# Attention and gated MLP on one core: one SBUF pool for raw q, k, v and for the weight conversions, with two weight pieces and part of x's sums moved beside the last two pairs

## The chip, the core and the metric

The kernel runs on one core of a Trainium2 chip. The metric is the device time of one execution in microseconds (us). The core has a matrix engine (PE, with its weight loads listed as PEld), a vector engine (DVE), an activation engine (ACT), a general engine (POOL) and SP, which here only issues DMA transfers. Each engine works through its own queue in order. Numbers of a profile come from one profiled execution; times are medians over several runs.

## What is computed

The reference has two parts. Attention over 8 images and 8 heads, 576 tokens and 64 channels per head, with a mask by blocks of 64; then a gated MLP over all 4608 tokens:

```python
scores = scale * np.matmul(q, k.transpose(0, 1, 3, 2))
mask = block_i >= block_j
scores = np.where(mask, scores, -1000000000.0)
scores = scores - np.max(scores, axis=-1, keepdims=True)
attn = np.exp(scores)
attn = attn / (np.sum(attn, axis=-1, keepdims=True) + 1e-09)
attn_out = np.matmul(attn, v)
x = attn_out.transpose(0, 2, 1, 3).reshape(B * S, H * D)      # 4608 x 512
gate = 1.0 / (1.0 + np.exp(-(x @ w_gate)))
out = gate * (x @ w_val) @ w_out                              # 512 -> 1536 -> 512
```

The three weights come in as 64-bit floats, q, k and v as 32-bit floats.

## The kernel before

**Arithmetic.** Wide products run in a rounded 32-bit format (F32R in the code). To keep precision, most operands are held as a high part and a low part (H and L in names), the high part by a copy that rounds, the low part by a subtraction; a product then takes three matmuls: high by high, high by low, low by high.

**Weights.** A 64-bit weight arrives as two 32-bit words (`raw`). `to_f32` (lines 650 to 673) makes a 32-bit float `cT` of them by integer operations on DVE: lines 659, 666, 668, 670, 672 and 673, with a mask of the small values made on ACT by a square (line 665), or on DVE (line 662) where the flag `alone` is set. `combine` (line 683) then forms sums of four weight blocks (lines 694 to 697) and splits them into high (ACT, line 698) and low parts (DVE, line 699). `wo_piece` (line 702) does the same for the output weights, without sums, and splits at lines 708 and 709. One call of either is a "piece"; a unit of weights, such as (0, 0) or (0, 1), has two pieces.

**First stage: attention and the first four of twelve hidden chunks.** 32 pairs (an image and two heads), numbered 0 to 31, run one after the other, in a software pipeline written out by hand (the loop at line 574): in its step p, the scores and softmax of pair p run beside the second half (transposes, product with v) of pair p-1 and `prep`, which loads and transposes q and k, of pair p+1. `convert` works off weight pieces for this stage, and `mlp1` computes the first four hidden chunks of an image whose attention is done; its matmuls are mixed into PE's queue by a rate. The loop has one step more than pairs: in step 32 only the second half of pair 31 is left. Then `run(mlp)` (line 829) works off what is left of `mlp1`, which for the last image, image 7, is nearly all. A tick is one part of such a step; p = 31 has some 22 of them.

**Second stage: the other eight hidden chunks.** It runs in two groups g of four hidden chunks, and within a group over k = 0 to 5, blocks of 768 tokens. The two products by w_gate and w_val use seven block products in place of eight (Strassen's scheme, in `unit`), so that x, too, has to be brought in as seven sums: `x_fetch` (line 711) loads four blocks of x from DRAM into `XB` (line 723) and makes three sums and, in slot 6, a fourth (lines 727 to 730), on DVE for the first block and on POOL for the others; `x_split` (lines 735 to 740) makes high (ACT, line 738) and low (DVE, line 739) parts in `XO`, the tiles `XH` and `XL`. `unit` issues the block products (line 749) and DVE and ACT clear the results (lines 765 to 793), with the low part of the hidden values at line 757. `out_block` multiplies by the output weights (line 807), and adds, in the second group, what the earlier parts left in DRAM (lines 821 to 824). Four units of 42 matmuls and an output part of 72 matmuls make a block.

**Order around the change.** The tile framework takes the program as written, adds every wait that data need, and orders each engine's queue by its own planner's simulation. `behind(a, b)` forces a after b on the same queue without a wait. Before, in the order of the program:

1. the loop over pairs ends, and the attention's pool `at` closes;
2. the pools `x2` (first weights, XO) and `cv` (raw weights, `cT`, `XB`) open, on the memory of `at`;
3. `combine` of unit (0, 0), both pieces (line 826), `x_fetch` and `x_split` of block 0 (line 827);
4. `run(mlp)`, whose first multiplication on DVE (line 135) is put behind the sums of step 3 (`first_sums`, lines 826 to 828, used at line 518);
5. `combine` of units (0, 1), (1, 0), (1, 1), then four pieces of the output weights, in the order 0, 2, 1, 3;
6. the loop over g and k, which fetches the x of the next block at its head.

In the first stage the raw rows of q, k and v lie in `rq`, `rk` and `rv`, the transposed ones in a buffer with the tag T, the split q in two tiles `QS0` and `QS1` by turns, and the keys in two buffers of `KD`. All of these belong to `at`. The low parts of k are made at line 251, on POOL from pair 1 on; a pair's keys then go to the other half of the partitions by a transfer within SBUF (line 252).

Of the kernel before, what the change touches and what calls it, by code (L numbers as in the profile page):

```python
# [9 lines left out]
F32 = mybir.dt.float32  # L10
# [8 lines left out]
F1 = 4  # L19
# [10 lines left out]
def attn_glu_kernel(ctx: ExitStack, tc: tile.TileContext, q, k, v, w_gate, w_val, w_out, out):  # L30
# [118 lines left out]
    with ExitStack() as s2:  # L149
        s1 = ExitStack()  # L150
        s_at = ExitStack()
        mp, xp1, wp1, xp0 = (s1.enter_context(tc.tile_pool(name=x, bufs=1, side="left")) for x in ("m1", "x1", "w1", "x0"))
        at = s_at.enter_context(tc.tile_pool(name="at", bufs=1, side="right"))
# [19 lines left out]
        QSs = [at.tile([P, 2, 640], F32R, name=f"QS{i}") for i in range(2)]  # L173
# [67 lines left out]
        def prep(p):  # L241


            KD = at.tile([P, 2, 2, S], F32R, name="KD", bufs=2)
            QS = QSs[p % 2]
            kT = at.tile([P, S], F32, name="kT", tag="T", bufs=1)
# [7 lines left out]
            qT = at.tile([P, S], F32, name="qT", tag="T", bufs=1)  # L254
# [304 lines left out]

        n = len(pairs)  # L560
# [12 lines left out]

        for p in range(n + 1):
            pr = prep(p + 1) if p + 1 < n else iter(())
# [11 lines left out]
            for g, what in plan:  # L587
# [7 lines left out]
                for _ in part:  # L595
# [9 lines left out]
                    convert_to(p, min(1.0, tick / 20))  # L605
            convert_to(p, 1.0)
# [12 lines left out]

        W_OF = {1: 0, 5: 1, 2: 2, 4: 3, 7: 4, 6: 5, 3: 6}
        X_OF = {1: 0, 7: 1, 2: 2, 3: 3, 5: 4, 6: 5, 4: 6}
        G = (NF - F1) // 4
        NK = NTOK // (2 * N2)
        KC = NC // 2
        def pool(name, **kw):  # L630
            return s2.enter_context(tc.tile_pool(name=name, bufs=1, side="right", reuse_waits="tile", **kw))
        units = [(q, gv) for q in range(2) for gv in range(2)]

        s_at.close()
        x2 = pool("x2")
        cv = pool("cv")
        wp = {(0, 0): x2}
        wgv_d = dram.tile([4, P, KC, 2, 7, P], F32, name="wgv_d")
        wo_d = dram.tile([P, 4, 2, DM], F32, name="wo_d")
        part2_d = dram.tile([NTOK, DM], F32, name="part2_d")  # L640
        last2 = {}

        def mark2(engine, ins):
            last2[engine] = ins.ins
# [6 lines left out]

        def to_f32(raw, T_, sq, held, alone=False):

            def after(engine, ins):
                if held and engine in last2:
                    behind(ins.ins, last2[engine])
            lo, hi = raw[:, :, 0], raw[:, :, 1]
            Tu = T_.bitcast(U32)
            after("DVE", nc.vector.tensor_scalar(out=Tu, in0=hi, scalar1=3, scalar2=0x3FFFFFF8,
                                                 op0=ALU.logical_shift_left, op1=ALU.bitwise_and))  # L660
            if alone:
                nc.vector.tensor_scalar(out=sq.bitcast(U32), in0=hi, scalar1=0x7FFFFFFF, scalar2=None,
                                        op0=ALU.bitwise_and)
            else:
                after("ACT", nc.scalar.activation(out=sq, in_=hi.bitcast(F32), func=AF.Square))
            nc.vector.scalar_tensor_tensor(out=Tu, in0=hi, scalar=0xC0000000, in1=Tu,
                                           op0=ALU.bitwise_and, op1=ALU.bitwise_or)
            nc.vector.scalar_tensor_tensor(out=T_, in0=sq, scalar=TINY_HI if alone else TINY_HI * TINY_HI, in1=T_,
                                           op0=ALU.is_ge, op1=ALU.mult)
            nc.vector.tensor_scalar(out=hi, in0=Tu, scalar1=0xFF800000, scalar2=None, op0=ALU.bitwise_and)  # L670
            Ef = hi.bitcast(F32)
# [253 lines left out]
```

## Time and profile before

| | us |
|---|---|
| median of 3 runs | 1315.14 (1311.15 to 1316.25) |
| the profiled execution | 1313.64 |
| its span, first to last instruction | 1311.8 |
| stage 1 with the attention's last work (the last x parts of pair 31 made) | to about 681 |
| first block product of the second stage | 731.1 |

The profile gives each engine's busy time, a chain of waits followed back from the last instruction, groups of instructions by source line with mean durations in ns, and, on request, instructions in order of time. In rows of the latter the first number is the start, the second the length, then the engine, the line of the kernel, the operation, and what it writes and reads (`out<-in`), with the count of merged instructions; idle time just before it stands in brackets with what ended it. SPq is SP's queue of transfer issues. A row of a chain has start, length and work.

For the whole span:

```profile
PE   5879899999999999999997969999999999999997
DVE  7899988989899898898849996887887757556643
PEclk8989989999999999999998979999999999999999
```

Each digit is a slice of a fortieth of the span, in tenths of busy time, or of full clock.

### The profile page before, as it was taken

The numbers are of one execution on the slowest core, as the hardware profiler recorded it, in microseconds if no ns is written. First come the engines' busy times: TensorE is split into PE (matmuls) and PEld (weight loads), VectorE is DVE, ScalarE is ACT, GpSimd is POOL, SyncE is SP. The second block draws the span as 40 slices with busy tenths as digits, with TensorE's granted clock in tenths as the row PEclk, the third lists the DMA queues.
The fourth block names the chain that finished last, engine by engine and source line by source line (L and its number), as shares of the span: only waits on it lengthen the run. The fifth ranks groups of instructions, "written<-read, shape, count | busy, mean of one in ns | idle before, by whom it ended". The sixth has DMA issues, their size and how long they took to land.

```text
span 1311.8 us, 21661 instructions
## 1 busy us (share of the span) xinstructions
PE 1226.5 (93%) x7312; PEld 1132.2 (86%) x7312; DVE 1044.9 (80%) x2097; ACT 781.0 (60%) x1871; POOL 506.8 (39%) x490
## 2 busy tenths in 40 slices
PE   5879899999999999999997969999999999999997
PEld 4668779989899898999997959899899999999996
DVE  7899988989899898898849996887887757556643
ACT  5877768888888888888855433444445324223320
POOL 2313344535545355454520134313322415624531
PEclk8989989999999999999998979999999999999999
DMA  7656535354454544544232334423528632542442
GB/s 144 141 122 137 123 80 130 79 128 92 88 123 83 125 91 102 113 82 114 70 94 78 121 120 166 141 92 138 173 85 315 234 96 98 193 152 74 161 145 97
DMA packets 256959, 161.87 MB, mean 123 GB/s; under 512 B 197328, under 2 KB 217808, under 8 KB 256208
## 3 DMA queue, kind: packets, MB, share of 16 engines
q1 hardware_dynamic: 255248, 157.53, 44.4%
q10 hardware_dynamic: 1600, 2.95, 0.6%
q8 instruction: 58, 0.95, 0.3%
q14 instruction: 53, 0.43, 0.1%
HBM read 94.37 MB, written 47.19 MB: 108 GB/s over the span
## 4 chain that ended last, share of the span: by engine, by line
PE 57%; DVE 24%; ACT 8%; DMA 6%; issue 3%; SPq 1%; POOL 0%; DVEq 0%; POOLq 0%; ACTq 0%
PE b L749 21%; PE bank L222 10%; PE m L114 6%; PE m L807 6%; PE m L123 5%; PE bank L225 3%; PE b L807 3%; DVE QS L260 2%; DVE P L371 2%; DVE XL L739 2%; DMA part_d<-ost 2%; ACT P L316 2%; DVE nm L324 2%; DMA rq<-in_q_dram 1%; PE bank L114 1%
## 5 line engine op out<-in xcount | busy, mean ns | idle before, releaser
L749 PE MATMUL b<-XH,w 128*128 128x384 f32 x1344 | 353.7, 339 | 12.2 <-ACT XH L738 6.7
L749 PEld LDWEIGHTS b<-XH,w 128*128 128x128 f32 x1344 | 245.8, 189 | 20.1 <-ACT XH L738 7.9
L749 PE MATMUL b<-XL,w 128*128 128x384 f32 x672 | 226.4, 337 | 1.3 <-DVE XL L739 1.3
L222 PE MATMUL bank<-KD,QS 128*128 128x288 f32 (+4 forms) x768 | 160.7, 332 | 17.0 <-DMA KD<-KD 11.3
L316 ACT ACTIVATE P<-bank,nm 128x512 f32<-128x512 f32 (+3 forms) x256 | 134.1, 528 | 29.4 <-DVE nm L324 18.4
L222 PEld LDWEIGHTS bank<-KD,QS 128*128 128x128 f32 x768 | 117.9, 197 | 26.1 <-DVE QS L260 11.3
L251 POOL TENSOR_TENSOR KD<-kT,KD 64x576 fp32r<-64x576 f32 x62 | 91.1, 1470 | 113.5 <-ACT KD L250 111.1
L749 PEld LDWEIGHTS b<-XL,w 128*128 128x128 f32 x672 | 127.1, 189 | 3.6 <-DVE XL L739 1.8
L807 PE MATMUL m<-wo,hH 128*128 128x512 f32 x384 | 125.4, 392 | 0.0
L225 PE MATMUL bank<-ident,P 128*128 128x128 f32 x640 | 96.3, 282 | 18.9 <-DVE P L371 10.9
L114 PE MATMUL m<-XH,wv 128*128 128x288 f32 x448 | 106.9, 305 | 3.8 <-DVE h L135 3.8
L822 POOL TENSOR_TENSOR pr<-pr,pr 128x512 f32<-128x512 f32 x36 | 46.9, 1305 | 156.6 <-DMA pr<-part_d 155.8
L114 PE MATMUL m<-XH,wg 128*128 128x288 f32 x448 | 105.3, 304 | 0.6 <-ACT t L133 0.5
L225 PEld LDWEIGHTS bank<-ident,P 128*128 128x128 f32 x640 | 76.2, 144 | 26.9 <-ACT P L316 14.5
L222 PE MATMUL bank<-G1H,VS 128*128 128x320 f32 (+2 forms) x352 | 95.6, 355 | 1.8 <-ACT G1H L295 1.8
L371 DVE TENSOR_SCALAR P<-P,sm 128x512 f32<-128x512 f32 (+3 forms) x256 | 91.2, 414 | 1.0
L807 PEld LDWEIGHTS m<-wo,hH 128*128 128x128 f32 x384 | 72.3, 189 | 13.8
L297 DVE TENSOR_TENSOR G1L<-bank,G1H 128x512 fp32r<-128x512 f32 (+1 forms) x120 | 74.2, 622 | 12.0 <-ACT G1H L295 11.5
L772 ACT ACTIVATE g<-g 128x384 f32<-128x384 f32 x72 | 37.0, 524 | 77.2 <-DVE g L785 66.5
L114 PEld LDWEIGHTS m<-XH,wv 128*128 128x128 f32 x448 | 76.8, 190 | 4.8 <-DVE h L135 4.6
L114 PEld LDWEIGHTS m<-XH,wg 128*128 128x128 f32 x448 | 76.5, 190 | 1.6 <-ACT t L133 1.3
L324 DVE TENSOR_REDUCE nm<-bank 128x1 f32<-128x384 f32 (+1 forms) x128 | 76.3, 603 | 0.8
(181 smaller groups left out, 3103.1 us busy)
## 6 DMA issues: line engine op xcount, KB each, us to landing
KD<-KD SPq DMA_DIRECT2D x64, 288.0 KB, 3.1
pr<-part_d SPq DMA_DIRECT2D x72, 256.0 KB, 3.6
part_d<-ost SPq DMA_DIRECT2D x60, 256.0 KB, 3.0
rk<-in_k_dram SPq DMA_DIRECT2D x128, 72.0 KB, 2.5
XB<-xT_d SPq DMA_DIRECT2D x16, 576.0 KB, 5.3
out_dram<-ost SPq DMA_DIRECT2D x36, 256.0 KB, 2.9
xT_d<-xT SPq DMA_DIRECT2D x30, 288.0 KB, 2.3
rv<-in_v_dram SPq DMA_DIRECT2D x64, 128.0 KB, 2.8
```

Source lines behind the costliest of these rows:

```text
L114: mm = nc.tensor.matmul(ps, lhsT=lh, rhs=rh, start=(i == 0), stop=(i == n - 1))
L123: mm = nc.tensor.matmul(ps, lhsT=lh[:, f, t * P:(t + 1) * P], rhs=rh, start=(i == 0), stop=(i == n - 1))
L222: pe_last[:] = [nc.tensor.matmul(*args, **kw).ins]
L225: pe_last[:] = [nc.tensor.transpose(*args).ins]
L251: (nc.gpsimd if p else nc.vector).tensor_sub(out=KD[s, h, 1], in0=kT[s], in1=KD[s, h, 0].bitcast(F32))
L297: mark("DVE", nc.vector.tensor_sub(out=dst[1], in0=src, in1=dst[0].bitcast(F32)))
L316: mark("ACT", nc.scalar.activation(out=Pi[:, h], in_=ps, func=AF.Exp, bias=nm[:, c0 + h:c0 + h + 1], accum_out=sm[:, c0 + h:c0 + h + 1]))
L324: mark("DVE", nc.vector.tensor_reduce(out=nm[:, c0 + h:c0 + h + 1], in_=ps, axis=AX.X, op=ALU.max, negate=True))
L371: mark("DVE", nc.vector.tensor_scalar_mul(Pi[:, h], Pi[:, h], sm[:, c0 + h:c0 + h + 1]))
L749: mm = nc.tensor.matmul(ps, lhsT=lh, rhs=rh, start=(first and k == 0), stop=(k == n - 1), skip_group_check=not first)
L807: mm = nc.tensor.matmul(po[t], lhsT=lh[:, f, t * P:(t + 1) * P], rhs=rh, start=(half == 0 and i == 0), stop=(half == 1 and i == 5))
L822: nc.gpsimd.tensor_add(out=pr[0], in0=pr[0], in1=pr[1])
```

## The change

Raw q, k, v, the transposed ones, `QS` and `KD` move from `at` into a pool `cv` that opens before `at` and stays for the rest of the kernel; there they are `rqk` (raw q and k), `rvT` (raw v, and behind it the transposed k or q), `QS0`, `QS1` and `KD`. The second stage's `raw` takes by turns the tags of `QS0` and `QS1`, its `cT` those of `rqk` and `rvT`, and `XB`, with six slots in place of seven, that of `KD`. The helpers that need them are defined before the loop over pairs. With that:

- at the start of steps 31 and 32 the raw words of one piece of unit (0, 0) and one half of block 0's x are fetched; the sums of the first piece are made at tick 20 of step 31, x's first three sums at tick 1 of step 32, the sums of the second piece at tick 4 of step 32, each behind the last marked DVE instruction of the attention;
- after the loop come the sums of x's second half, the splitting of the two pieces, high part now on DVE, and then fetch and sums of unit (0, 1), its mask on DVE; the low parts of block 0's x are put behind these; line 135's first multiplication waits in order only for the sums of x's second half;
- x's slot 6 is no longer made with the sums: `x_split` subtracts in place on DVE in slot 2, after slots 0 to 3 have been split, and splits in three parts in place of two;
- block 1's x is loaded after unit (0, 1) has been split, and its sums are made on DVE, behind the last instruction of unit (1, 0); later blocks' sums stay on POOL.

```diff
+        cv = s2.enter_context(tc.tile_pool(name="cv", bufs=1, side="right", reuse_waits="tile"))
...
-        rq = at.tile([P, S], F32, name="rq")
-        rk = at.tile([P, S], F32, name="rk")
-        rv = at.tile([P, 5, P], F32, name="rv")
+        rqk = cv.tile([P, 2, S], F32, name="rqk")
+        rq, rk = rqk[:, 0], rqk[:, 1]
+        rvT = cv.tile([P, 5 * P + S], F32, name="rvT")
+        rv, qkT = rvT[:, :5 * P].rearrange("p (t d) -> p t d", d=P), rvT[:, 5 * P:]
...
-        QSs = [at.tile([P, 2, 640], F32R, name=f"QS{i}") for i in range(2)]
+        QSs = [cv.tile([P, 2, 640], F32R, name=f"QS{i}") for i in range(2)]
...
-            KD = at.tile([P, 2, 2, S], F32R, name="KD", bufs=2)
+            KD = cv.tile([P, 2, 2, S], F32R, name="KD", bufs=2)
...
-            kT = at.tile([P, S], F32, name="kT", tag="T", bufs=1)
+            kT = qT = qkT
...
+        def cv_tiles():
+
+            i = n_cv[0] % 2
+            n_cv[0] += 1
+            return (cv.tile([P, 4 * P, 2], U32, name="raw", tag=f"QS{i}"),
+                    cv.tile([P, 8, P], F32, name="cT", tag=("rqk", "rvT")[i]))
...
+        def split_gv(T, dst, alone=False):
+            if alone:
+                nc.vector.tensor_copy(out=dst[:, 0], in_=T[:, :7])
+            else:
+                nc.scalar.copy(out=dst[:, 0], in_=T[:, :7])
+            return nc.vector.tensor_sub(out=dst[:, 1], in0=T[:, :7], in1=dst[:, 0].bitcast(F32)).ins
...
+        def x_load(k, j):
...
+            XB = cv.tile([P, 6, N2], F32, name="XB", tag="KD", bufs=2)
...
+        def x_sums(XB, eng, other=None):
+            t1 = eng.tensor_sub(out=XB[:, 4], in0=XB[:, 1], in1=XB[:, 0])
+            if other:
+                behind(t1.ins, other)
+            eng.tensor_sub(out=XB[:, 1], in0=XB[:, 3], in1=XB[:, 1])
+            return eng.tensor_sub(out=XB[:, 5], in0=XB[:, 3], in1=XB[:, 4]).ins
+
+        def x_split(XBs, other=None):
+
+            def split(a, b, src):
+                for j, XB in enumerate(XBs):
+                    if src == 2:
+                        nc.vector.tensor_sub(out=XB[:, 2], in0=XB[:, 2], in1=XB[:, 5])
+                    x = XB[:, src:src + b - a]
+                    nc.scalar.copy(out=XO[j][0][:, a:b], in_=x)
+                    sub = nc.vector.tensor_sub(out=XO[j][1][:, a:b], in0=x, in1=XO[j][0][:, a:b].bitcast(F32))
+                    if other:
+                        behind(sub.ins, other)
+
+            split(0, 4, 0)
+            split(4, 6, 4)
+            split(6, 7, 2)
...
+        def early_work(p, tick):
+
+            when = p - (n - 1), tick
+            if when in ((0, 0), (1, 0)):
+                early.append(fetch_gv(0, 0, 0, len(early)))
+                early_x.append(x_load(0, len(early_x)))
+            if when == (0, 20):
+                sums_gv(*early[0], alone=last["DVE"])
+            if when == (1, 1):
+                x_sums(early_x[0], nc.vector, last["DVE"])
+            if when == (1, 4):
+                sums_gv(*early[1], alone=last["DVE"])
...
-        first_sums = [combine(0, 0, 0, j, W[0, 0][:, j], alone=True) for j in range(KC)]
-        x_split(x_fetch(0, nc.vector))
-        first_sums.append(last2["T4"])
+        first_sums = [x_sums(early_x[1], nc.vector)]
+        for j in range(KC):
+            done = split_gv(early[j][1], W[0, 0][:, j], True)
+        early = [fetch_gv(0, 0, 1, j) for j in range(KC)]
+        for e in early:
+            sums = sums_gv(*e, alone=done)
+        x_split(early_x, sums)
         run(mlp)
...
-        for q, gv in units[1:]:
+        for n, (q, gv) in enumerate(units[1:]):
             for j in range(KC):
-                combine(0, q, gv, j, W[q, gv][:, j])
+                if n:
+                    done = combine(0, q, gv, j, W[q, gv][:, j])
+                else:
+                    split_gv(early[j][1], W[q, gv][:, j])
+            if n == 1:
+                sums_after = done
+            if n == 0:
+                XBs = [x_load(1, j) for j in range(KC)]
         for f in (0, 2, 1, 3):
             wo_piece(0, f, wo[:, f])
+        for XB in XBs:
+            x_sums(XB, nc.vector, sums_after)
...
-                if not end:
-                    XBs = x_fetch((k + 1) % NK, nc.gpsimd)
+                if not end and (g or k):
+                    XBs = [x_load((k + 1) % NK, j) for j in range(KC)]
+                    for XB in XBs:
+                        x_sums(XB, nc.gpsimd)
```

`fetch_gv` and `sums_gv` are the fetching and summing parts of the former `combine`, `early_work` is called at the head of each step and after each tick.

More of the change, by code (lines that the diff above doesn't have):

```diff
@@ L558, in mlp1, with pool @@
                         queue.dma_start(out=part_d[r:r + 64, :], in_=ost[64 * j:64 * j + 64, :])
+        W_OF = {1: 0, 5: 1, 2: 2, 4: 3, 7: 4, 6: 5, 3: 6}
+        X_OF = {1: 0, 7: 1, 2: 2, 3: 3, 5: 4, 6: 5, 4: 6}
+        G = (NF - F1) // 4
+        NK = NTOK // (2 * N2)
+        KC = NC // 2
+        def pool(name, **kw):
+            return s2.enter_context(tc.tile_pool(name=name, bufs=1, side="right", reuse_waits="tile", **kw))
+        units = [(q, gv) for q in range(2) for gv in range(2)]
@@ new lines, in fetch @@
+        def fetch(raw, src, held):
+            for dst, x in zip(raw, src):
+                d = nc.sync.dma_start(out=dst, in_=x.bitcast(U32))
+                if held:
+                    behind(d.ins, last2["SP"])
+                else:
+                    mark2("SP", d)
+        n_cv = [0]
+        def cv_tiles():
[3 more added lines that the diff above has]
+                    cv.tile([P, 8, P], F32, name="cT", tag=("rqk", "rvT")[i]))
@@ new lines, in x_load @@
+        def x_load(k, j):
+            b, o = divmod(2 * k * N2, S)
+            n0 = S - o
+            XB = cv.tile([P, 6, N2], F32, name="XB", tag="KD", bufs=2)
+            v = XB[:, 0:4].rearrange("p (kh th) n -> p kh (th n)", kh=2)
+            src = xT_d.rearrange("b (kh c p) s -> c b p kh s", kh=2, c=KC)[j]
+            for dst, x in ((v[:, :, :n0], src[b][:, :, o:]), (v[:, :, n0:], src[b + 1][:, :, :2 * N2 - n0])):
+                d = nc.sync.dma_start(out=dst, in_=x)
+                if "SP" in last2:
+                    behind(d.ins, last2["SP"])
+                mark2("SP", d)
+            return XB
@@ L650, in attn_glu_kernel @@
         XO = [[x2.tile([P, 7, N2], F32R, name=f"X{e}{j}") for e in "HL"] for j in range(KC)]
[L652 to L671, printed above, removed]
-            nc.vector.scalar_tensor_tensor(out=Ef, in0=lo, scalar=2.0 ** -52, in1=Ef, op0=ALU.mult, op1=ALU.mult)
-            nc.vector.tensor_add(out=T_, in0=T_, in1=Ef)
@@ L735, in x_split @@
-        def x_split(XBs):
-            for a, b in ((0, 4), (4, 7)):
-                for j, XB in enumerate(XBs):
-                    nc.scalar.copy(out=XO[j][0][:, a:b], in_=XB[:, a:b])
-                    nc.vector.tensor_sub(out=XO[j][1][:, a:b], in0=XB[:, a:b],
-                                         in1=XO[j][0][:, a:b].bitcast(F32))
         def product(i, ps, w, first):
```

127 lines of the change are left out of this document (58 added, 69 removed).

## The prediction

> **What bounds the kernel now.** I read the page's busy times and chain first, then busy time by stage, then PE's timeline in the stages where PE is not full.
>
> ```profile
> PE 1226.5 (93%) x7312; PEld 1132.2 (86%) x7312; DVE 1044.9 (80%) x2097; ACT 781.0 (60%) x1871; POOL 506.8 (39%) x490
> PE 57%; DVE 24%; ACT 8%; DMA 6%; issue 3%; SPq 1%; POOL 0%; DVEq 0%; POOLq 0%; ACTq 0%
> 660.00:676.00 16.00, 16.00 (x114) 15.29 (x114) 9.99 (x25) 9.83 (x27) 5.22 (x6) 1.00 0.11 36
> 676.00:687.00 11.00, 11.00 (x63) 9.76 (x62) 0.69 (x2) 3.51 (x7) 2.16 (x2) 1.00 0.63 184
> 687.00:731.00 44.00, 35.99 (x217) 33.43 (x216) 40.15 (x89) 21.67 (x37) 0.00 (x0) 0.92 0.32 107
> 731.00:790.00 59.00, 48.63 (x236) 44.39 (x235) 58.34 (x89) 25.14 (x41) 19.61 (x15) 0.88 0.35 115
> 790.00:835.00 45.00, 44.66 (x233) 41.09 (x232) 34.52 (x55) 19.61 (x34) 13.47 (x12) 1.00 0.35 115
> ```
>
> In the stage rows the columns after the length are PE, PEld, DVE, ACT and POOL busy, then PE's granted clock and the DMA share. PE is full at 660-687 and 790-835. It is not between: there DVE is full (58.34 of 59.00), straight after it did almost nothing for 11 us (0.69). So over the change's place DVE sets the pace. PE's timeline shows the price, the idle time in brackets:
>
> ```profile
> 703.02 0.61 PE L114 MATMUL bank<-XH,wg 128*128 128x288 f32 x1 [8.01 <-DVE h L135]
> 760.63 0.44 PE L749 MATMUL b<-XH,w 128*128 128x384 f32 x1 [2.22 <-DVE g L785]
> 773.47 0.44 PE L749 MATMUL b<-XH,w 128*128 128x384 f32 x1 [3.42 <-ACT XH L738]
> 776.96 1.33 PE L749 MATMUL b<-XH,w 128*128 128x384 f32 x3 [3.05 <-ACT XH L738]
> 782.05 0.69 PE L749 MATMUL b<-XL,w 128*128 128x384 f32 x1 [1.27 <-DVE XL L739]
> 700.00:705.00 5.00, 1.98 (x8) 1.98 (x9) 5.00 (x11) 3.01 (x8) 0.00 (x0) 0.50 0.00 0
> 705.00:710.00 5.00, 5.00 (x34) 5.00 (x33) 5.00 (x14) 2.12 (x6) 0.00 (x0) 0.84 0.01 3
> 760.00:765.00 5.00, 4.37 (x15) 4.00 (x16) 5.00 (x11) 3.07 (x7) 0.00 (x0) 0.66 0.63 204
> 775.00:780.00 5.00, 2.84 (x8) 2.33 (x9) 5.00 (x4) 2.63 (x2) 4.92 (x4) 0.50 0.00 0
> 780.00:785.00 5.00, 3.73 (x11) 2.96 (x12) 5.00 (x5) 1.77 (x2) 0.77 (x1) 0.50 0.34 97
> ```
>
> **First stall:** 8.0 idle, and work at a lowered clock, 1.98 x 0.50 + 5.00 x 0.16 = 1.8, together 9.8 us. **Second stall:** 2.22 + 3.42 + 3.05 + 1.27 = 10.0 idle, and 4.37 x 0.34 + 2.84 x 0.50 + 3.73 x 0.50 = 4.8, together 14.8. So 24.6 us is all that the change can win here.
>
> Why DVE is late stands in its own rows, in the DVE groups and in SP's queue:
>
> ```profile
> L727 DVE TENSOR_TENSOR XB<-XB 128x384 f32<-128x384 f32 x2 | 1.1, 557 | 11.3 <-DMA XB<-xT_d 11.3
> 651.36 16.83 SPq L677 DMA_DIRECT2D raw<-in_moe_w_gate_dram  x4
> 677.53 8.17 SPq L723 DMA_DIRECT2D XB<-xT_d  x4
> 671.05 0.42 DVE L659 TENSOR_SCALAR cT<-raw 128x512 uint32<-128x512 uint32 x1
> 675.75 0.68 DVE L668 SCALAR_TENSOR_TENSOR cT<-cT 128x512 f32<-128x512 f32 x1
> 688.74 1.48 ACT L738 CAST XH<-XB 128x1536 fp32r<-128x1536 f32 x1 [1.23 <-DVE XB L728]
> 691.42 0.55 DVE L730 TENSOR_TENSOR XB<-XB 128x384 f32<-128x384 f32 x1
> 786.66 2.92 DVE L709 TENSOR_TENSOR wo<-cTo,wo 128x512 fp32r<-128x512 f32 x2
> ```
>
> DVE waits 11.3 us for x's first sums, whose loads SP issues only from 677.53: their memory belongs to the attention's pool until then. The x they load is images 0 and 1, written long ago. The last output weights are done at 786.66 + 2.92 = 789.6; that end is the mark I move.
>
> **The change part by part, on DVE's queue.**
>
> *x's loads and two weight pieces go early (gain 11.3).* The new tiles take memory of the previous pair's keys, queries and raw inputs, free once that pair's scores are done, so the 11.3 us wait has nothing left to wait for. SP issues these eight transfers earlier, with nothing but the four raw loads from 651.36 to move past.
>
> *Sums beside the last two pairs (gain 5.3).* One piece costs:
>
> ```profile
> 720.55 0.75 DVE L659 TENSOR_SCALAR cT<-raw 128x512 uint32<-128x512 uint32 x2
> 727.92 0.48 DVE L697 TENSOR_TENSOR cT<-cT 128x128 f32<-128x128 f32 x2
> 674.21 0.41 DVE L662 TENSOR_SCALAR cT<-raw 128x512 uint32<-128x512 uint32 x1
> 719.11 1.08 DVE L699 TENSOR_TENSOR w<-cT,w 128x896 fp32r<-128x896 f32 x1
> ```
>
> The first two rows begin and end the sums of two pieces, back to back: 728.40 - 720.55 = 7.85, so 3.9 each, and 0.34 more where the mask is made on DVE (the third row, less the overlap with its neighbour): 4.3. Two pieces are 8.5; before, the ten operations from 671.05 to 676.43 did 4.9 of that (5.4 less 0.5 in one slow operation), so 3.6 leaves the time after 687, and x's first three sums with it (3 x 0.56 by the L727 row = 1.7). They need 10.2 us of DVE's time before 676. There it has 16.00 - 9.99 = 6.0 idle, and 5.0 from those ten operations. That fits, but with little over.
>
> *New on DVE (loss 6.7).* Two copies for the first weights, which ACT made before: the trace has no DVE copy. Nearest are the 512-wide one-input row at 0.41 (0.72 if stretched to 896) and the 896-wide subtraction at 1.08; I take 0.7, between 0.4 and 1.1 each: 1.4. The Trainium skill ("VectorE: DVE Perf Modes", "The perf-mode tier table") has fp32 copies in SBUF at two elements a cycle, 1227 ns for 2048; worked down to 896 that is an estimate of 0.6, and the sum would be 0.2 better. Two masks of the second unit: 0.7. Block 1's x sums, moved here from POOL: 6 x 0.55 = 3.3. The last slot of x is now subtracted in the split, which has three subtractions in place of two: 0.1 for block 0, and for block 1, where POOL did it, 2 x 0.55 + 0.1: 1.2.
>
> *POOL off DVE's back (gain 6.4).*
>
> ```profile
> 769.28 1.24 POOL L727 TENSOR_TENSOR XB<-XB 128x384 f32<-128x384 f32 x1 [12.99 <-DMA XB<-xT_d]
> 779.44 1.33 POOL L730 TENSOR_TENSOR XB<-XB 128x384 f32<-128x384 f32 x1
> 769.57 1.50 DVE L668 SCALAR_TENSOR_TENSOR cTo<-cTo 128x512 f32<-128x512 f32 x1
> 774.80 2.54 DVE L739 TENSOR_TENSOR XL<-XB,XH 128x1536 fp32r<-128x1536 f32 x1
> 779.84 2.15 DVE L739 TENSOR_TENSOR XL<-XB,XH 128x1152 fp32r<-128x1152 f32 x1
> 783.12 1.74 DVE L739 TENSOR_TENSOR XL<-XB,XH 128x1536 fp32r<-128x1536 f32 x1
> 739.23 22.77 SPq L677 DMA_DIRECT2D raw<-in_moe_w_out_dram  x4
> 762.09 20.80 SPq L723 DMA_DIRECT2D XB<-xT_d  x6
> ```
>
> While POOL makes block 1's eight sums (769.28 to 780.77), eight DVE operations in a row, from 769.57 to 779.84, are each about 0.8 longer than their like: 2.54 against 1.74 at 783.12. Eight times 0.8 is 6.4, and it goes with POOL's sums. The Trainium skill ("SBUF — State Buffer", "Who interferes with whom") calls this an exclusive lock, in which the later of the two waits for the other's whole instruction. By that rule up to POOL's 11.5 us could come back; the sum would be 5.1 better, and a lengthening of 0.8 against POOL's 1.24 fits a lock that had partly run out. The rule also speaks against the change: early sums with two inputs lie beside POOL's work for the last pair. The last two rows show SP: block 1's x queues behind the output weights until 762; in the new order its loads are issued ahead of the later units' weights.
>
> *New waits (loss 2.5).* What is queued behind the early sums on DVE is pair 31's softmax and transposed copies, and PE's transposes wait for those. If the 6.0 idle is filled and the rest pushes, pair 31 ends 10.2 - 6.0 = 4.2 later. PE can fill with image 6's output products (below, its last one). The first weights' split now writes memory of the attention's pool, and waits for the last pair's buffers. And the weights' raw buffers are still two, so a load can show once DVE is ahead:
>
> ```profile
> 684.82 0.39 PE L123 MATMUL m<-wo,hH 128*128 128x512 f32 x1
> 761.67 5.15 DMA raw<-in_moe_w_out_dram
> ```
>
> Bounds 0 and 4.2 + 5.15 = 9.4; I take 2.5, nearer to nothing, since the same load cost DVE little before. If all the cover went, the gain would fall by 6.9 more.
>
> *At nothing:* one pool for q, k and v keeps the same number of buffers and the same order of reads and writes. The ten later x blocks each get 1.2 more on DVE and two POOL sums less; this lies beside the output products, 72 matmuls of a chunk, with PE full and DVE at 34.52 of 45.00 at 790-835. Without that cover it costs 10 x 1.2 = 12.
>
> **Sum:** -11.3 - 5.3 + 6.7 - 6.4 + 2.5 = -13.8, under the cap of 24.6. The profiled execution took 1313.6 (span 1311.8 and 1.8 around it), so 1299.8; it lies 1.5 under the median, by which it is 1301.3. I forecast 1300, between the two. Its own range, with the copies, the waits and half of the contention unsure, is 1292 to 1307. The first stall should go almost wholly, the second shrink to some 11 us.
>
> **The rivals.**
>
> *Both stalls go wholly:* -24.6, so 1289.0, by the median 1290.5. For it: every stall is owed to DVE or to x's late loads. Against it: DVE has no slack at 731-790, and 14 us of lead don't cover PE's earlier start.
>
> *Only the first goes:* 9.8 less the 4.2 by which pair 31 may slip is 5.6, so 1308.0, by the median 1309.5. It holds if the second unit's sums, now ahead of the last image's activations, or bare loads eat the lead before 770. For it: the 5.15 load in the chain.
>
> *The early work isn't early:* if the loads wait for the pool, or the planner sets the sums behind the last pair, the wait moves and nothing is won: 1311 to 1318. Against it: the tiles' former owners are done a pair earlier.
>
> *Slower:* q and k become halves of one tile, and v and the transposed q and k another. If waits are kept by tile, and not by region, each pair's transposes of k wait for q's loads, at lines 247 and 211. A load of q lands in about 2 us:
>
> ```profile
> 587.68 2.07 DMA rq<-in_q_dram
> ```
>
> Over 30 pairs that is up to 62 us; it decides from about half a microsecond a pair (30 x 0.5 = 15), where it eats the gain. With two thirds hidden by PE's filling it is 62 / 3 - 14 = 7 slower, 1320, and up to 1361. Against it: the cast of XB's slots 0 to 3 began at 688.74, before slot 6 of that tile was written (691.42), so regions are told apart.
>
> **How the numbers follow.** Forecast 0.50; both stalls 0.14; first only 0.16; not early 0.10; slower 0.10. A measurement can tell 0.5%, 6.6 us, from no change. Faster by that, under 1308.6: 0.49 + 0.14 + 0.05 = 0.68; within it: 0.20; slower: 0.12, with the tail of the rest. The range reaches from inside the both-stalls case to the end of the not-early case, 1288 to 1318, and leaves out most of the slower case.
>
> **What would show it.** x's first loads and the first raw weights issued before 662; no 10 us hole in DVE at 676-687; no PE idle of 8 us before the last image's products; the last output weights done near 775; no POOL sums of x and no 1.5 us L668 there. It is wrong if the pairs before 31 take longer, if DVE waits on a DMA among the last pair's work, or if PE idles at another place in the first block for the same sum.

## The result and the profile after

| | before | after |
|---|---|---|
| median | 1314.32 us (1311.15 to 1316.25, 4 runs) | 1302.52 us (1299.63 to 1303.52, 4 runs) |
| ratio | | 0.9909, 95% interval 0.9883 to 0.9935 |
| the profiled execution, span | 1311.8 | 1300.8 |

A second set of the changed kernel gave 1300.12 us and 0.9880 (0.9865 to 0.9895). So one set places this kernel to about 0.3%, and that has to be kept in mind with every comparison below. All eight runs of the two sets lie between 1297.2 and 1303.5, with a median of 1300.6.

The page's busy line and the stage rows of the changed kernel come first, with the same columns as before: length, then PE, PEld, DVE, ACT and POOL busy, PE's clock, DMA share and GB/s.

```profile
PE 1223.1 (94%) x7312; PEld 1128.6 (87%) x7312; DVE 1031.6 (79%) x2153; ACT 782.0 (60%) x1891; POOL 480.3 (37%) x462
660.00:676.00 16.00, 14.81 (x108) 13.90 (x106) 16.00 (x34) 8.30 (x23) 6.08 (x6) 1.00 0.32 102
676.00:687.00 11.00, 11.00 (x62) 9.64 (x61) 9.42 (x21) 4.48 (x10) 4.47 (x4) 1.00 0.45 146
687.00:731.00 44.00, 41.40 (x256) 38.15 (x254) 32.63 (x72) 19.70 (x38) 1.31 (x1) 1.00 0.42 138
731.00:790.00 59.00, 54.11 (x278) 50.96 (x279) 58.42 (x106) 26.63 (x47) 11.71 (x10) 0.94 0.25 83
790.00:835.00 45.00, 42.45 (x210) 37.68 (x209) 32.32 (x62) 20.55 (x36) 13.37 (x11) 1.00 0.49 164
```

DVE's empty stretch at 676 to 687 is filled: 9.42 us of work where there were 0.69. PE gains 5.4 us of work at 687 to 731 and 5.5 at 731 to 790, at a higher clock. It loses 1.2 at 660 to 676 and 2.2 at 790 to 835. Where PE now idles stands in its timeline, and what its clock did in windows of 5 us (columns: length, PE busy, clock, DMA share, GB/s):

```profile
669.86 0.41 PE L228 MATMUL bank<-ident,P 128*128 128x128 f32 x2 [0.83 <-DVE P L373]
725.37 0.45 PE L794 MATMUL b<-XH,w 128*128 128x384 f32 x1 [1.41 <-ACT ost L552]
732.11 0.56 PE L794 MATMUL b<-XH,w 128*128 128x384 f32 x1 [2.30 <-ACT ost L552]
760.16 0.69 PE L794 MATMUL b<-XH,w 128*128 128x384 f32 x1 [2.49 <-DVE g L830]
812.35 0.44 PE L794 MATMUL b<-XH,w 128*128 128x384 f32 x1 [2.55 <-DVE v L830]
730.00:735.00 5.00, 2.39 (x7) 0.73 0.25 62
735.00:740.00 5.00, 5.00 (x29) 0.93 0.00 0
755.00:760.00 5.00, 2.67 (x16) 0.96 0.00 0
760.00:765.00 5.00, 4.84 (x18) 0.70 0.28 97
```

The five rows idle for 9.6 us, and three short ones (670.64, 733.81, 769.43) for 0.37 + 0.50 + 0.62 = 1.5 more: 11.1 in all. The lowered clock cost 2.39 x 0.27 + 5.00 x 0.07 + 2.67 x 0.04 + 4.84 x 0.30 = 2.6. Together that is 13.7. The kernel before, counted in the same way (waits of 0.3 us and more, from 655 to 900), idled 18.8 us and lost 6.6 to the clock: 25.4. So 11.7 went, and the span fell by 11.0, which is to say that PE's idle time and clock around the hand-over account for the gain to about 1 us. The first stall of 8.0 us is gone; the second became several small ones.

A measure that the experiments below need follows from this. Let the hand-over be the time from the transposes of the last pair's q on DVE to the first product of block 3 of the second stage. It was 248.7 us before (627.4 to 876.1), 237.2 after (628.2 to 865.4), and 236.5 in the profile of the second set. What lies behind block 3's first product took from 433.7 to 438.5 us in all these profiles, and differs by 1.7 us between the two of the changed kernel itself. So a time alone can hide, or feign, a few us of the hand-over.

The other engines show something else. These are DVE's first wait with the work of POOL, PE and ACT ahead of it, DVE's second wait, the transfers of the last image's output tiles in the chain of waits (start, length), and the ends of the work in question:

```profile
692.23 0.46 DVE L135 SCALAR_TENSOR_TENSOR h<-t,bank 128x288 f32<-128x288 f32 x1 [6.75 <-ACT t L133]
686.87 1.44 POOL L461 TENSOR_TENSOR XL<-xT,XH 128x576 fp32r<-128x576 f32 x1 [0.79 <-ACT XH L458]
690.57 0.29 PE L114 MATMUL bank<-XH,wg 128*128 128x288 f32 x1
690.83 0.30 PE L114 MATMUL bank<-XH,wv 128*128 128x288 f32 x1
691.75 0.39 ACT L133 ACTIVATE t<-bank 128x288 f32<-128x288 f32 x1
687.04 4.32 ACT L692 CAST XH<-XB 128x1536 fp32r<-128x1536 f32 x4 [0.24 <-ACT XH L458]
727.42 2.09 DVE L648 TENSOR_TENSOR w<-cT,w 128x896 fp32r<-128x896 f32 x2 [4.45 <-ACT w L647]
721.23 3.40 DMA part_d<-ost
725.35 6.03 DMA part_d<-ost
773.58 1.02 DVE L693 TENSOR_TENSOR XL<-XB,XH 128x384 fp32r<-128x384 f32 x2
788.32 0.68 DVE L662 TENSOR_TENSOR wo<-cT,wo 128x512 fp32r<-128x512 f32 x1
```

DVE no longer waits for x, but it waits 6.75 us for the last image's first tanh and 4.45 us for a cast of weights: 11.2 us in place of the 11.3 that went. ACT makes x's casts (4.32 us) ahead of the tanh, but that is a small part of it: the two PE rows end image 7's first gate and first value product, at 690.9 and 691.1 (PE's first two signals after 688.4 in the trace), and the multiplication needs both, so ACT's order can have cost 1.1 us at most. PE comes to them that late because these products end with the last pair's x, whose low part POOL has ready at 688.3. In the kernel before, POOL and ACT did the same at

```profile
679.41 1.43 POOL L459 TENSOR_TENSOR XL<-xT,XH 128x576 fp32r<-128x576 f32 x1 [0.79 <-ACT XH L456]
685.74 0.41 ACT L133 ACTIVATE t<-bank 128x288 f32<-128x288 f32 x1
```

so the tanh now comes 6.0 us later, and nearly all of DVE's first wait is the last pair's lateness. The weights' cast stands on ACT behind output tiles that wait for one of two staging tiles, which two transfers of 3.40 and 6.03 us hold. So the last output weights are done at 788.32 + 0.68 = 789.0, against 789.6 before: the mark did not move. What did move is block 1's x. Its last low part is done at 773.58 + 1.02 = 774.6. In the kernel before, DVE's row for it is

```profile
785.39 1.34 DVE L739 TENSOR_TENSOR XL<-XB,XH 128x1152 fp32r<-128x1152 f32 x1
```

which ends at 786.7, 12 us later. In the changed kernel PE therefore has products to do between 775 and 785, without a pause and at full clock. The first of the two windows:

```profile
775.00:780.00 5.00, 5.00 (x30) 1.00 0.94 315
```

In the kernel before, the same two windows held 2.84 and 3.73 us of work at half clock.

### The profile page after: what moved, and what is told of

It is laid out like the page before. It is cut to its first block, busy times and chain, and to the rows that moved or that the text cites. A ratio compares the mean times of both kernels' runs of the same rounds, so it can differ in the third digit from the quotient of the medians.

```text
span 1300.8 us, 21669 instructions
## 1 busy us (share of the span) xinstructions
PE 1223.1 (94%) x7312; PEld 1128.6 (87%) x7312; DVE 1031.6 (79%) x2153; ACT 782.0 (60%) x1891; POOL 480.3 (37%) x462
## 4 chain that ended last, share of the span: by engine, by line
PE 57%; DVE 23%; ACT 7%; DMA 6%; issue 3%; POOL 3%; SPq 1%; DVEq 0%; POOLq 0%; ACTq 0%
PE b L794 18%; PE bank L225 9%; PE m L852 8%; PE m L114 6%; PE m L123 5%; PE b L852 4%; PE bank L228 3%; DVE QS L262 2%; DVE P L373 2%; PE bank L114 2%; DMA pr<-part_d 2%; ACT P L318 2%; DVE nm L326 2%; ACT KD L253 1%; DVE G1L L299 1%
## 5 line engine op out<-in xcount | busy, mean ns | idle before, releaser
L794 PE MATMUL b<-XH,w 128*128 128x384 f32 x1344 | 354.0, 338 | 11.7 <-ACT ost L552 3.7
L225 PE MATMUL bank<-KD,QS 128*128 128x288 f32 (+4 forms) x768 | 160.5, 331 | 17.2 <-DMA KD<-KD 11.3
L225 PEld LDWEIGHTS bank<-KD,QS 128*128 128x128 f32 x768 | 117.4, 196 | 26.3 <-DVE QS L262 11.3
L254 POOL TENSOR_TENSOR KD<-rvT,KD 64x576 fp32r<-64x576 f32 x62 | 90.9, 1467 | 112.0 <-ACT KD L253 109.6
L228 PE MATMUL bank<-ident,P 128*128 128x128 f32 x640 | 97.0, 283 | 20.6 <-DVE P L373 11.8
L692 ACT CAST XH<-XB 128x1536 fp32r<-128x1536 f32 (+2 forms) x72 | 65.9, 938 | 32.4 <-DVE XB L690 22.6
L852 PEld LDWEIGHTS m<-wo,hH 128*128 128x128 f32 x384 | 71.9, 188 | 13.7
L299 DVE TENSOR_TENSOR G1L<-bank,G1H 128x512 fp32r<-128x512 f32 (+1 forms) x120 | 74.3, 622 | 11.8 <-ACT G1H L297 11.4
L679 POOL TENSOR_TENSOR XB<-XB 128x384 f32<-128x384 f32 x20 | 28.1, 1406 | 145.0 <-DMA XB<-xT_d 99.1
```

The lines of the kernel that those rows point to most:

```text
L225: pe_last[:] = [nc.tensor.matmul(*args, **kw).ins]
L228: pe_last[:] = [nc.tensor.transpose(*args).ins]
L254: (nc.gpsimd if p else nc.vector).tensor_sub(out=KD[s, h, 1], in0=kT[s], in1=KD[s, h, 0].bitcast(F32))
L299: mark("DVE", nc.vector.tensor_sub(out=dst[1], in0=src, in1=dst[0].bitcast(F32)))
L692: nc.scalar.copy(out=XO[j][0][:, a:b], in_=x)
L794: mm = nc.tensor.matmul(ps, lhsT=lh, rhs=rh, start=(first and k == 0), stop=(k == n - 1), skip_group_check=not first)
```

## The experiments

Theory A is the prediction's: DVE's queue behind the pairs is the limit, and its length gives the time. The rivals name other limits: block 1's x (e3), the last pair that the early sums push (e1), the staging tiles (e4, e7). Times are medians; each ratio is taken against the kernel before on the same chip. The hand-over is that of the one profiled execution; the last two columns say when the work named was done.

| run | edit to the changed kernel | us | ratio, 95% interval | hand-over | last output weights | last of block 1's x |
|---|---|---|---|---|---|---|
| e10 | none | 1300.12 | 0.9880, 0.9865 to 0.9895 | 236.5 | 788.9 | 774.5 |
| e1 | no early sums | 1305.32 | 0.9934, 0.9911 to 0.9956 | 238.5 | 790.3 | 775.3 |
| e11 | no early work in the text | 1305.33 | 0.9920, 0.9905 to 0.9935 | 239.5 | 792.9 | 777.8 |
| e3 | block 1's x loaded late | 1302.55 | 0.9915, 0.9899 to 0.9930 | 240.6 | 783.9 | 784.4 |
| e4 | five staging tiles, memory of image 6's x | 1312.78 | 0.9988, 0.9977 to 0.9998 | 249.2 | 801.2 | 788.2 |
| e7 | four staging tiles, memory of image 7's x | 1300.87 | 0.9887, 0.9866 to 0.9908 | 237.5 | 788.7 | 773.1 |
| e2 | block 1's x sums on POOL | 1299.48 | 0.9880, 0.9861 to 0.9900 | 236.1 | 784.5 | 774.9 |
| e5 | second unit's sums first | 1297.83 | 0.9873, 0.9856 to 0.9890 | 232.4 | 771.9 | 771.3 |
| e12 | e5 and e2 | 1300.67 | 0.9888, 0.9875 to 0.9901 | 237.0 | 771.7 | 776.7 |
| e9 | e5 and e1 | 1296.32 | 0.9863, 0.9839 to 0.9887 | 230.7 | 773.9 | 772.9 |
| e8 | e5 and e7 | 1297.30 | 0.9861, 0.9839 to 0.9884 | 232.9 | 773.8 | 773.2 |
| e13 | e5, e1 and e7 | 1296.79 | 0.9869, 0.9849 to 0.9889 | 230.8 | 773.3 | 772.2 |

### The changed kernel again

> The changed kernel itself, once more, beside the two below on the same chip. Its first look gave 0.9909 of the time before, with an interval from 0.9883 to 0.9935; in the stretch from the last pair's transposes (628.2) to the end its profile has 672.6 us. Expected: 0.990 to 0.991, 1301.5 to 1303.5 us.

It came out a little below what was expected, a miss by 0.2%. Its profile repeats the first one: DVE's holes are 6.74 and 4.32, and PE idles 10.0 us in all at 655 to 900, against 11.1.

### The early sums (e1, e11)

```diff
-            if when == (0, 20):
-                sums_gv(*early[0], alone=last["DVE"])
-            if when == (1, 1):
-                x_sums(early_x[0], nc.vector, last["DVE"])
-            if when == (1, 4):
-                sums_gv(*early[1], alone=last["DVE"])
...
+        for e in early:
+            sums_gv(*e, alone=last["DVE"])
+        x_sums(early_x[0], nc.vector)
         first_sums = [x_sums(early_x[1], nc.vector)]
```

> The changed kernel with its early loads kept, but the sums of the first two weight pieces and x's first three sums made after the pairs instead of beside the last two. Theory A (the prediction: DVE's queue after the pairs is the limit, and the early sums take 5.3 us out of it): about 5 us slower than the changed kernel, some 1307 to 1308. Rival B (the early sums only push the last pair, which ends 7 us later with them, and DVE then idles 6.75 us where the last image's first activations come late): the pair ends 5 to 7 us earlier, the 6.75 us hole fills with the sums, and the time is within 2 us of the changed kernel, 1301 to 1304.

e11 moves the loads behind the pairs too (`fetch_gv` and `x_load` beside these sums):

> The changed kernel with no early work in its text: the first two raw pieces, x's first loads and all their sums stand behind the pairs, as before the change; only the shared memory and the rest stay. Theory A (it is the shared memory that lets x's loads go early: nothing has to wait for the attention's pool): SP still issues x's loads before 662, the 11.3 us wait stays away, and the time is that of the run without the early sums, 1304 to 1306. Rival (the place in the text does it): the loads come behind 676 again, DVE waits some 10 us for x, PE's 8 us stall is back, and the time is 1311 to 1315.

Both gave 1305.3 us, 3 to 5 above the changed kernel's two sets, which is theory A's side. The intervals overlap that of the first set, and not that of the second, which ran on the same chip as e11. But the hand-over is only 1.3 to 2.0 us longer in e1 and 2.3 to 3.0 in e11; the rest of the 3 to 5 lies behind block 3's first product, where no edit explains it. So the early sums are worth less here than the times say.

The first half of e1's rival holds. The last product of the last pair, counted from the transposes of its q, starts after 50.1 us without the early sums (626.74 to 676.80) and after 55.0 with them (628.21 to 683.23); before the change it was 49.1 (627.38 to 676.46). So they do push the pair, by 5 us. That the last x part of the pair is nevertheless no earlier (its last POOL operation starts 59.9 us after the transposes in e1, 58.7 in the changed kernel, 52.0 before) has its cause on POOL. This is the same POOL operation, a low part of image 6's hidden values, before the change, in the changed kernel and in e1:

```profile
671.63 0.70 POOL L141 TENSOR_TENSOR hL<-h,hH 128x224 fp32r<-128x224 f32 x1 [1.36 <-ACT hH L140]
676.47 2.59 POOL L141 TENSOR_TENSOR hL<-h,hH 128x224 fp32r<-128x224 f32 x1 [1.72 <-ACT hH L140]
676.77 8.13 POOL L141 TENSOR_TENSOR hL<-h,hH 128x224 fp32r<-128x224 f32 x1 [3.89 <-ACT hH L140]
```

In e1 DVE works without a pause until 684.4, and the operation ends at 684.9; the pair's last two POOL operations stand behind it. So e1 does not leave the last pair in peace: it trades a late product for a held POOL, and DVE's hole shrinks to 3.78 us but is not filled.

e11 shows what let the loads go early. In its profile SP still issues x's first loads from 642.9 on, though their text stands behind the pairs. It is the shared memory that does it. With no early work in its text e11 also keeps most of the gain (0.9920, and 9.2 of 11.5 us of the hand-over).

### Which of the two late works counts (e3)

```diff
-            if n == 0:
-                XBs = [x_load(1, j) for j in range(KC)]
         for f in (0, 2, 1, 3):
             wo_piece(0, f, wo[:, f])
+        XBs = [x_load(1, j) for j in range(KC)]
```

> The changed kernel with the loads of block 1's x put behind the output weights' loads, as before the change; the sums stay on DVE. Theory A (the mark is the end of the last output weights, and x of block 1 lies beside it): within 1.5 us of the changed kernel, with the mark at the same place. Rival B (the gain of the second half of the stage is that block 1's x is split by 775 in place of 785): PE stalls again before block 1, 3 to 8 us of idle with the clock at half behind it, and the time is 6 to 10 us slower than the changed kernel, 1308 to 1312.

Both theories were half right. PE's idle time before block 1 in e3 stands first below, and then DVE's last work:

```profile
771.02 0.44 PE L794 MATMUL b<-XH,w 128*128 128x384 f32 x1 [2.98 <-ACT XH L692]
774.15 0.69 PE L794 MATMUL b<-XL,w 128*128 128x384 f32 x1 [1.47 <-DVE XL L693]
782.64 1.28 DVE L662 TENSOR_TENSOR wo<-cT,wo 128x512 fp32r<-128x512 f32 x2
783.84 0.55 DVE L693 TENSOR_TENSOR XL<-XB,XH 128x384 fp32r<-128x384 f32 x1
```

The stalls before block 1 are back, as B said (4.5 us). The output weights are done 5.1 us earlier (783.9), x 9.8 later (784.4), and the waits of 2.49 at 760 and 2.55 at 812 are down to 1.4 or gone. The time is that of the changed kernel's first set, and 2.4 us above its second; the hand-over decides, and is 3.4 to 4.1 us longer. So loading block 1's x early is worth that much, about half of what B said, while theory A's mark came earlier. The two works change places on DVE, but not for nothing.

### The staging tiles (e4, e7)

```diff
+            osts = []
+            if b == B - 1:
+                o4 = xp0.tile([P, 4, DM], F32, name="ost7", tag="XH0")
+                osts = [o4[:, t] for t in range(4)] + [xp0.tile([P, DM], F32, name="ost7t", tag="XL0")]
...
-                ost = mp.tile([P, DM], F32, name="ost", bufs=2)
+                ost = osts[t] if osts else mp.tile([P, DM], F32, name="ost", bufs=2)
```

> The changed kernel with five output staging tiles of their own for the last image, in the memory of the image before it, in place of the two shared ones. The three waits for a staging tile (5.9 us on ScalarE) go in any case. If PE's order of work is what bounds the stage from 725 on: the idle 1.41 + 2.30 us and the lowered clock behind it (about 1.7) go, and the time falls by 3 to 5 us, to 1298 or so. If the output weights' queue on DVE bounds it: the 4.45 us hole on DVE goes and the gain is up to 4 as well, but then with the last output weights done before 786. If neither (PE only waits later for the same thing): within 1 us of the changed kernel, with the idle time behind 760 larger by what went.

This missed by far, in a way that none of the three cases had. ACT's and DVE's rows of e4:

```profile
728.66 1.78 ACT L651 CAST w<-cT 128x896 fp32r<-128x896 f32 x2 [1.98 <-DMA part_d<-ost7t]
726.77 0.56 DVE L829 TENSOR_TENSOR g<-b,p 128x384 f32<-128x384 f32 x1 [13.13 <-ACT p L814]
```

The second unit's weights take the memory that the staging tiles now held, so their cast waits for the last staging transfer, and the block's first addition was set ahead of them on DVE, which then stood for 13.13 us. The edit tested its own side effect, and its time is near that of the kernel before (0.9988). e7 takes `tag="XH1"` in `xp1`, the last image's own x, for four tiles:

> The changed kernel with four output staging tiles of their own for the last image, this time in the memory of the last image's own x (read last by the products just before), which the second unit's weights don't take, unlike the memory of the image before. If the three waits for a staging tile are a price of the change: PE's idle 1.41 + 2.30 us at 724 to 732 and the clock behind it go, DVE's 4.45 us hole goes, and the time falls by 3 to 5 us, to 1298 or so. If PE and DVE only wait later for the same work: within 1.5 us of the changed kernel. As slow as the run with five tiles (1313) only if it was the order of the instructions, not the weights' memory, that made that one slow.

The two idle times of PE at 724 to 732 are gone in its profile, as is the 13 us hole, but others came: 1.65 at 741, 1.42 at 744, 1.71 at 759, 2.90 at 809. DVE's 4.45 is down to 3.17. PE's idle total is 10.8, the time lies between the changed kernel's two sets, and the hand-over is within 1 us of both. "PE and DVE only wait later for the same work" held: the output weights end at 788.7, where they did.

### The order of DVE's queue (e5, e9, e8, e13)

```diff
         for e in early:
             sums = sums_gv(*e, alone=done)
+            first_sums.append(sums)
```

`first_sums` is what line 135's first multiplication is put behind.

> The changed kernel with the second unit's sums set ahead of the last image's first gated product on DVE, so that DVE does them in its 6.75 us hole. Theory A (DVE's queue is the limit): the hole shrinks below 1.5 us, the last output weights are done 4 to 6 us earlier and the time falls by 4 to 6 us, to 1297 or so. Rival B (the output weights are not what ends last; block 1's x and PE's own waits are): the hole goes, and the time stays within 2 us of the changed kernel. Slower by 1 to 3 if the last image's activations now come late for its output products.

Rows of POOL and DVE in e5, from the stretch in which DVE idles in the changed kernel, and its last output weights:

```profile
682.44 7.31 POOL L451 TENSOR_TENSOR xT<-u,tt 128x256 f32<-128x256 f32 x1 [5.27 <-ACT u L447]
688.68 0.49 DVE L641 TENSOR_TENSOR cT<-cT 128x128 f32<-128x128 f32 x2
692.20 1.76 DVE L693 TENSOR_TENSOR XL<-XB,XH 128x1536 fp32r<-128x1536 f32 x1 [3.04 <-ACT XH L692]
771.24 0.68 DVE L662 TENSOR_TENSOR wo<-cT,wo 128x512 fp32r<-128x512 f32 x1
```

The sums run to 689.2, where DVE stood still before; of 6.75 us of idle time 3.04 are left, and 1.50 soon after. The 4.45 us hole is gone with it, since the cast it waited for comes off ACT before the output tiles. The mark is at 771.9: 17 us earlier, near the 775 that the prediction had wanted from the change itself. The time fell by 2.3 to 4.7 us, near theory A's 1297, and the hand-over by 4.1 to 4.8, not by the mark's 17: PE had little idle time left to lose (8.3 us at 655 to 900). And 5.0 of these 8.3 are new. The sums in DVE's hole hold POOL: its step for the last pair's x takes 7.31 us in place of the changed kernel's 1.43, ends 0.6 us after DVE's sums do, and PE then stands for 3.07 us at 690.5 for that x and for 1.63 at 697.7 for the tanh behind it.

> The sums ahead of the last image's first gated product, but none beside the last two pairs: all the first pieces' sums come after the pairs. It tells what the early sums are worth once DVE's hole is used otherwise. If they fill idle time of DVE before 676 (the prediction's 5.3 us): 4 to 6 us slower than the run with the sums ahead alone (1297.8), 1302 to 1304. If the pair they push costs as much as they save: within 1.5 us of it. The 2.8 us that leaving them out cost without this edit would be 1300.6.

The early sums are worth nothing any more: 1296.32, and PE idles 5.5 us, 2.1 of them at the place of e5's 5.0. The hand-over is 1.7 us shorter without them, and 2.1 in the pair e13 and e8. They fill DVE's time before 676, but the hole of 6.75 held room for as much, and they push the last pair, as e1 showed.

> Both edits: staging tiles in the last image's x, and the second unit's sums ahead of the last image's first gated product. In the run with the sums ahead alone PE has no idle left at 724 to 732, though the three waits for a staging tile stand (5.3 us on ScalarE). If they are then hidden: within 1.5 us of that run (1297.8). If they still hold DVE's queue back: 2 to 4 us faster, 1294 to 1296.

1297.30, within 1.5 us of e5: the staging waits are hidden, as ACT now makes the weights' cast ahead of the output tiles.

> The second unit's sums ahead of the last image's first gated product, no sums beside the last two pairs, and the staging tiles in the last image's x. The two runs with the first of these edits and one of the others stand at 0.9861 and 0.9863 of the time before. If the order of DVE's queue behind the pairs is what the changed kernel still loses: 0.985 to 0.988 again, 1295 to 1299 us, below the changed kernel's two sets (0.9909 and 0.9880), with no DVE idle over 3 us at 676 to 787, the last output weights done near 773 and less than 6 us of PE idle at 655 to 900. If those runs were only a good draw: 0.988 to 0.991, 1300 to 1303. Staging waits that still cost would show as 2 to 3 us below 0.986.

1296.79, as the first case had it: no DVE idle over 3 us, the mark at 773.3, and 5.8 us of PE idle. The four kernels with this edit took 1295.5 to 1303.0 in 19 runs, median 1297.3, against 1300.6 for the changed kernel's eight: some 3 us faster than the change, 17 to 18 faster than before. The four sets lie below both sets of the changed kernel, but each interval overlaps one of those at least, and no record shows one of them beside the changed kernel on one chip. e8 and e9 did run beside e2 and e7, which are near the changed kernel, and their medians lie below both; the hand-over of all four is 3.6 to 6.5 us shorter than the changed kernel's.

### POOL beside DVE (e2, e12)

```diff
         for XB in XBs:
-            x_sums(XB, nc.vector, sums_after)
+            x_sums(XB, nc.gpsimd, sums_after)
```

> The changed kernel with block 1's six x sums on POOL again, at the same place in the order (behind the third unit's weights); the subtraction of the last slot stays on DVE. If POOL's operations lengthen DVE's as in the kernel before (0.8 us each, six to eight of them, 4.8 to 6.4 us, against 3.3 us of DVE's own work saved): 1.5 to 3 us slower than the changed kernel, 1304 to 1305.5, with DVE operations of 1.2 to 1.5 us beside POOL's sums. If the lengthening costs nothing there (or DVE isn't the limit): 0 to 3.3 us faster, 1299 to 1302.5.

The ratio, 0.9880, is at or a little below the changed kernel's, so the sums cost no more on POOL than on DVE there. POOL made them from 717 to 728, mostly in DVE's 4.23 us hole from 721. That could hide a price, so e12 puts them beside a DVE without that hole:

> The second unit's sums ahead of the last image's first gated product, and block 1's x sums on POOL. In the run with the POOL sums alone these ran at 717 to 726, inside DVE's 4.45 us hole, and cost DVE nothing: it was 1 to 3 us faster than the changed kernel. With the sums ahead that hole is gone and DVE is busy there. If POOL's work lengthens a busy DVE (the prediction's 0.8 us an operation): 1 to 3 us slower than the run with the sums ahead alone, 1298.5 to 1301. If not: up to 3 us faster than it, 1294.5 to 1297.

The first fence has rows of POOL and DVE in e12, the second DVE's same operations in e5, without POOL:

```profile
712.62 1.56 POOL L679 TENSOR_TENSOR XB<-XB 128x384 f32<-128x384 f32 x1 [1.51 <-DMA XB<-xT_d]
715.26 1.01 POOL L683 TENSOR_TENSOR XB<-XB 128x384 f32<-128x384 f32 x1
713.23 1.20 DVE L141 TENSOR_TENSOR hL<-h,hH 128x224 fp32r<-128x224 f32 x1
714.35 1.03 DVE L141 TENSOR_TENSOR hLt<-h,hHt 128x64 fp32r<-128x64 f32 x1
715.67 2.58 DVE L608 TENSOR_TENSOR cT<-cT,raw 128x512 f32<-128x512 f32 x2
718.17 1.26 DVE L141 TENSOR_TENSOR hL<-h,hH 128x288 fp32r<-128x288 f32 x1
```

```profile
711.88 0.38 DVE L141 TENSOR_TENSOR hL<-h,hH 128x224 fp32r<-128x224 f32 x1
712.18 0.22 DVE L141 TENSOR_TENSOR hLt<-h,hHt 128x64 fp32r<-128x64 f32 x1
712.68 1.29 DVE L608 TENSOR_TENSOR cT<-cT,raw 128x512 f32<-128x512 f32 x2
713.88 0.45 DVE L141 TENSOR_TENSOR hL<-h,hH 128x288 fp32r<-128x288 f32 x1
```

The lengthening is there: 0.82 + 0.81 + 1.29 + 0.81 = 3.7 us in these five operations, more than the 3.3 that the prediction gave the sums themselves on DVE. Block 1's x is done 5.4 us later than in e5 (776.7), and the time is 1300.67, 2.8 above it: the side of the prediction's term. The intervals, taken on two chips, overlap by 0.0015, but the hand-over is 4.6 us longer than in e5, so the price is on the path there.

## Why the prediction came out as it did

It forecast 1300 and the time was 1302.5 (1300.1 in the second set), faster as said, and inside the likeliest case's own range. By its steps:

**x's loads, -11.3.** Right that the wait goes: the loads went out from 643.0, and no DVE operation waits for them. Wrong that DVE's queue moves up by it. Two holes of 6.75 and 4.45 us took its place.

**Early sums, -5.3.** Leaving them out cost 1.3 to 2.0 us of the hand-over in the kernel as built, and saved 1.7 to 2.1 with the queue reordered (e9, e13). The step took the queue as a sum in which any work moved ahead counts in full; it counts only where no hole behind it would have held it. It also had the price on the last pair in another term, below, and that price was about as large.

**New on DVE, +6.7.** The two copies took 1.15 us together, against 1.4; the other parts were not measured apart. The Trainium skill ("VectorE: DVE Perf Modes", "The perf-mode tier table") gave an estimate of 0.6 each; this row agrees:

```profile
679.78 1.15 DVE L645 CAST w<-cT 128x896 fp32r<-128x896 f32 x2
```

**POOL off DVE's back, -6.4.** The price of 0.8 an operation is real (e12), but in the changed kernel it was not on the path: put back on POOL, block 1's sums cost nothing (e2). e12 differs from e2 in that DVE's hole is filled, and there they do. Nor did POOL leave DVE's back. With block 1's x split earlier, it makes block 2's sums from 778.7 to 786.3 (before the change from 786.6), beside the last output weights. Four DVE operations of 0.68 us took 1.51, 1.04, 1.50 and 1.03 there, 2.4 us more, against the sign that the prediction gave. The first of them:

```profile
781.09 1.51 DVE L607 SCALAR_TENSOR_TENSOR raw<-raw 128x512 f32<-128x512 uint32 x1
```

The prediction's remark that the early sums lie beside POOL's work for the last pair came true: the 0.70 us of POOL above became 2.59. By the rule that the Trainium skill gives ("SBUF — State Buffer", "Who interferes with whom"), the later engine waits for the other's whole instruction. On DVE the traces agree with a lock, but with less than a whole instruction: 0.65 to 0.82 beside POOL's 1.0 to 1.6. On POOL it was far more than one instruction of DVE: the 8.13 us of e1 span more than ten.

**New waits, +2.5, bounds 0 and 9.4.** This is the term that was mis-sized: DVE's two waits measured 11.2, beyond its upper bound. The first wait that it named did come. The early sums push the last pair's products by 5.0 us (e1), near the forecast 4.2, and with POOL's part its x is 6.6 us later than before. PE filled that time with image 6, as the prediction said. What it missed is that DVE, now ahead, meets the multiplication that needs this very x, and stands for 6.75 us. The second, 4.45, it had not named: a weights' cast stands on ACT behind output tiles that lack a staging tile.

**The mark at 775.** With 11.2 in place of 2.5 the prediction's sum is -5.1, and with nothing for POOL +1.3; the mark went from 789.6 to 789.0. That the time still fell by 11.8 is not the sum's doing: the number came out near the forecast by luck. What PE gained has other causes. Block 1's x was split 12 us earlier, which the prediction had only in a half sentence, and e3 gives it 3.4 to 4.1 us. And line 135's first multiplication came at 692.23 in place of 702.52, which ends the first stall.

What freed that multiplication stays open. Before the change it stood right behind the sums of the second weight piece, which ended at 702.6, by the order that the text asks for. The change drops that condition, and x's sums, the only one left, ended at 693.3 before. So the new order alone, with the old pools, might have ended most of the first stall; no run has the one without the other.

**The stalls.** The first went wholly, as forecast; the second was to shrink to some 11 and left 7.3 + 2.55 idle and 2.55 of clock, 12.4. That is several waits at other places of the first blocks, though not for the same sum as before. Of the rivals, slower by waits between q and k did not come: the last pair's transposes came at 628.2, against 627.4.

## What to carry to other kernels

When a wait on a full in-order engine goes, look at the first instructions behind it and ask what each of them waits for; an engine's queue moves up only to the next instruction whose input is late. Don't take the end of one queue's work for the time: e5 moved the mark by 17 us and the hand-over by 4 to 5. Before you fill an engine's idle time, ask whose work ran in it; here POOL's did. And before giving a buffer other memory, look who takes that memory next.

## What the runs showed of the hardware that was not expected

DVE's lengthening beside POOL is 0.65 to 0.82 us in the operations of e12, and does not grow with their length: 0.22 became 1.03, 0.38 became 1.20, 0.45 became 1.26. So short operations suffer most, in proportion.

It works the other way too, and more strongly. A POOL operation that starts beside a DVE working without a pause ends only when DVE pauses. The 0.70 us operation took 8.13 us in e1, e9, e11 and e13, and the last pair's transposed x, 0.74 us before the change, took 7.3 in e5, e8 and e12; in all seven the end came 0.5 to 0.6 us after DVE's first pause. Spans on POOL are rough, but PE agrees: in e1 it waits for the operation's result until 684.96. In e2 the first two sums of block 1's x met the same, until DVE's hole at 721.4, and the next took 0.99 us:

```profile
717.06 6.16 POOL L679 TENSOR_TENSOR XB<-XB 128x384 f32<-128x384 f32 x2 [30.35 <-DVE raw L605]
723.19 0.99 POOL L682 TENSOR_TENSOR XB<-XB 128x384 f32<-128x384 f32 x1
```
